# Every float32r matmul reads the two halves of its moving operand in turn

## The chip, the cores and the metric

The kernel runs on one core of one Trainium2 chip. The metric is the device time of one execution in microseconds (us); shown is the median of three executions. A profile of one further execution gives the durations that are read below; times in its rows are us unless marked ns. PE is the matmul engine (TensorE), PEld its weight load, which runs beside the matmuls; ACT is ScalarE, DVE VectorE, POOL GpSimd, SP the engine that starts the DMA transfers.

## The reference

Attention with a sigmoid in place of the softmax, and behind it a two-layer network with a squared ReLU. All inputs and outputs are float32.

```python
scores = scale * np.matmul(q, k.transpose(0, 1, 3, 2)) - np.log(S)   # 8 x 12 heads, S = 448, head_dim 64
attn = 1.0 / (1.0 + np.exp(-scores))
x = np.matmul(attn, v)            # -> 3584 tokens x 768
h = x @ w_in                      # 768 x 2048
r = np.maximum(h, 0.0)
out = (r * r) @ w_out             # 2048 x 768
```

## The kernel before

Precision comes from splitting. A float32 operand is cast to float32r, the fast matmul type, as a "hi" part (on ACT in `split_to`, L373, or on DVE, L566), and DVE subtracts that from the raw words for the "lo" part (L375, L377, L570). A product is then three float32r matmuls: hi by hi, hi by lo, lo by hi.

**Attention** (the first 246 us) goes over 24 blocks, function `block`; one block does two head pairs of one batch. A pair's two heads lie on partitions 0 to 63 and 64 to 127, so that the matmuls of the two heads run side by side. On PE a block is, in order: `scores_rest` (L322, 8 plain float32 matmuls for the last 64 keys of each head), `scores` of both pairs (L305, 36 float32r matmuls of 448 columns, that is 18 side-by-side pairs), then `attn_v` (L337) and `attn_v_rest` (L349) in plain float32. On ACT each of the score tiles passes through a sigmoid (L290): first the tile "rest", then six tiles "at". The sums of `attn_v` take the PSUM buffers that the sigmoids set free, in rotation over four. Beside that, ACT, DVE and POOL convert weights from 64-bit words and DVE adds up blocks for the matrix products.

**The two matrix products** use a seven-product (Strassen-like) scheme over halves of rows and columns, `gemm1` and `gemm2`, for four groups of tokens: three of 2 x 512 and a last one of 2 x 256 (`GROUPS`, T is 512 or 256). In the groups with T = 512 each matmul moves 512 columns: in `gemm1` the attention result (tiles xh, xl, xht, xlt, y, yt) against weights w1A to w1D, in `gemm2` the squared activations (tiles o_0h to o_3l). In the last group `gemm1` moves 256 columns (`product`), or, for products 2, 7 and 4, hi and lo side by side as 512 columns (L626) and then hi alone as 256 (L628, both in `joined_product`); `gemm2` is turned there: the activations are the stationary operand and the weights move, 384 columns at a time.

A moving operand of exactly 512 columns outside `joined_product` is read "woven" before the change: column 0 of the first half, column 0 of the second half, column 1 of the first, and so on. So that the result comes out in the plain order, `weave_to` and `split` write these operands with the raw words read at a step of two (even ones into the first half, odd ones into the second). All other matmuls read their moving operand from front to end, and their operands are split in plain order.

The order of the work is written out by hand for attention and for parts of the matrix products (`tc.manual_schedule`), and follows the program's order; PE results in `gemm1` are copied out of PSUM by ACT ("s", L688) before the next product adds onto the same bank.

Of the kernel before, what the change touches and what calls it, by code (L numbers as in the profile page):

```python
# [18 lines left out]
B, H, S, D = 8, 12, 448, 64  # L19
DM, DFF = H * D, 2048  # L20
P = 128
NP = H // 2

NT, KR = S // P, S % P
NF = DFF // P
NI = NF // 2
HALF = DM // 2
NE = HALF // P
GROUPS = ((0, 512), (1024, 512), (2048, 512), (3072, 256))
NG = len(GROUPS)  # L30
NS = 512
# [49 lines left out]
def sigmoid_attention_relu2_mlp(  # L81
# [47 lines left out]
    nc = tc.nc  # L129
# [3 lines left out]
    def op2(name, dtype=F32, n=S):  # L133
        return sb.tile([P, 2, n], dtype, tag="op2", bufs=N2, name=name)

    def op1(name, dtype=F32, n=S):
        return sb.tile([P, n], dtype, tag="op1", bufs=N1, name=name)
# [2 lines left out]
        return sb.tile([P, PH, HALF], dtype, tag="w", bufs=NW, name=name)  # L140

    def load_unit(src, u, name):
        t = wide(name).rearrange("p a n -> p (a n)")
        nc.sync.dma_start(out=t.bitcast(I32), in_=src[u].bitcast(I32))
        return t.rearrange("p (n w) -> p n w", w=2)
# [122 lines left out]
    def raw_of(half, k):  # L270
        if (half, k) not in raw_first:
            raw_first[half, k] = op2(f"x0_{half}{k}", n=NS), op1(f"y0_{half}{k}", n=NS)
        return raw_first[half, k]
# [14 lines left out]
    def sigmoid(name, sc):  # L288
        at = op2(name)
        nc.scalar.activation(at, sc, AF.Sigmoid, bias=NEG_LOG_S, scale=SCALE)  # L290
        return at

    def scores(b, p, x, passes=SPLIT, apart=0):

        sc, out = {}, []
        order = [range(apart), range(apart, len(passes))]
        for t, ns in [(t, order[0]) for t in range(NT) if apart] + [(t, order[1]) for t in range(NT)]:
            if t not in sc:
                sc[t] = two(f"sc_{b}_{p}_{t}")
            ks = slice(t * P, (t + 1) * P)  # L300
            for n in ns:
                kp, qp = passes[n]
                for j in range(2):
                    rows = slice(j * D, (j + 1) * D)
                    nc.tensor.matmul(  # L305
                        sc[t][:, j],
                        x[kp][rows, 1, ks],
                        x[qp][rows, 0],
                        start=(n == 0),
                        stop=(n == len(passes) - 1),  # L310
                    )
            if ns[-1] == len(passes) - 1:
                out.append(sigmoid(f"at_{b}_{p}_{t}", sc[t]))
        return out

    def scores_rest(d, xs):

        sc = two(f"sr_{d}")
        for r, x in enumerate(xs):
            for j in range(2):  # L320
                rows = slice(j * D, (j + 1) * D)
                nc.tensor.matmul(  # L322
                    sc[r * KR : (r + 1) * KR, j], x[rows, 1, NT * P :], x[rows, 0], start=True, stop=True
                )
        return sigmoid(f"rest_{d}", sc)

# [45 lines left out]
    def split_to(hi, lo, raw, later=None):  # L372
        nc.scalar.copy(out=hi, in_=raw)  # L373
        if later is None:
            nc.vector.tensor_sub(out=lo, in0=raw, in1=hi.bitcast(F32))  # L375
        else:
            later.append(lambda: nc.vector.tensor_sub(out=lo, in0=raw, in1=hi.bitcast(F32)))  # L377

    def unwoven(t, order):
        a = "a " if len(t.shape) > 2 else ""  # L380
        return t.rearrange(f"p {a}({order}) -> p {a}n s", n=2)

    def weave_to(hi, lo, raw, later=None):
        split_to(unwoven(hi, "n s"), unwoven(lo, "n s"), unwoven(raw, "s n"), later)

    def woven(t):
        return t.rearrange("p (n s) -> p s n", n=2)

    def split(raw, name, new):
        hi, lo = new(name + "h", F32R), new(name + "l", F32R)  # L390
        weave_to(hi, lo, raw)
        return hi, lo

    def x_operands(g):

        raw = {}
        t0, T = GROUPS[g]

        def load(n, b, k):
            if g == 0:
                raw[n] = raw_of(b, k)
                return
            r2, r1 = op2(f"x{n}_{g}", n=T), op1(f"y{n}_{g}", n=T)
            src = xd[3 * k : 3 * k + 3, :, t0 + b * T : t0 + (b + 1) * T].rearrange("c p s -> p c s")
            nc.sync.dma_start(out=r2, in_=src[:, 0:2])
            nc.sync.dma_start(out=r1, in_=src[:, 2])
            raw[n] = [r2, r1]

        def sub(n, a, b):
            for o, x, y in zip(raw[n], raw[a], raw[b]):
                nc.vector.tensor_sub(out=o, in0=x, in1=y)

        ops, ys = {}, {}

        def make(product, n, later=None, whole=False):
            if 2 * T > NS:
                y = op2(f"y{n}_{g}", F32R, T)
                h1, l1 = y[:, 0], y[:, 1]  # L420
                h2, l2 = (op2(f"{c}{n}_{g}", F32R, T) for c in ("xh", "xl"))
                ops[product] = [(h2[:, c], l2[:, c], None) for c in range(2)] + [(h1, l1, None)]
            else:
                x = op2(f"xj{n}_{g}", F32R, 2 * T)
                kind, at = SPOT[product]
                if kind not in ys:
                    ys[kind] = op2(f"yj{kind}_{g}", F32R, 2 * T)
                y = ys[kind][:, at]
                (h2, l2), (h1, l1) = ((t[..., :T], t[..., T:]) for t in (x, y))
                ops[product] = [(h2[:, c], l2[:, c], x[:, c]) for c in range(2)] + [(h1, l1, y)]  # L430
            (x2, x1) = raw[n]
            to = weave_to if 2 * T > NS else split_to
            to(h2, l2, x2, later)
            if whole:
                later.append(lambda: to(h1, l1, x1))
            else:
                to(h1, l1, x1, later)

        load("11", 0, 0)
        load("12", 1, 0)  # L440
        load("22", 1, 1)
        load("21", 0, 1)
        raw["t2"] = raw["22"] if g == 0 else [op2(f"xt_{g}", n=T), op1(f"yt_{g}", n=T)]
        raw["t1"], raw["t3"], raw["t4"] = raw["12"], raw["11"], raw["21"]
        return ops, {
            1: lambda *later: make(1, "11", *later),
            2: lambda *later: make(2, "21", *later),
            "t1": lambda: sub("t1", "12", "11"),
            "t2": lambda: sub("t2", "22", "t1"),
            6: lambda *later: make(6, "t2", *later),  # L450
            "t3": lambda: sub("t3", "t2", "11"),
            7: lambda: make(7, "t3"),
            5: lambda: make(5, "t1"),
            3: lambda *later: make(3, "22", *later),
            "t4": lambda: sub("t4", "21", "t2"),
            4: lambda: make(4, "t4"),
        }
# [5 lines left out]
    last = len(pairs) - 1  # L463
    todo = [(m, i) for m in range(2) for i in range(NI) if m == 0 or i not in DEFERRED]
    x, vt, xs, at, pav, xo, f64, w = {}, {}, {}, {}, {}, {}, {}, {}
    ready, stores, later, words = [], [], [], []
# [105 lines left out]
    def score(n, *args):  # L572
        at[n] = scores(*pairs[n], *args)
# [12 lines left out]
    first = {}  # L586
# [22 lines left out]
    def two(name):  # L609
        return duo(name, pools[next(turn) % 4])  # L610
# [4 lines left out]
    def product(out, w, c, x, first, last):  # L615
        (wh, wl), (xh, xl) = w, x
        for n, (a, b) in enumerate(((wh, xh), (wh, xl), (wl, xh))):
            moving = woven(b) if b.shape[-1] == NS else b
            nc.tensor.matmul(  # L619
                out, a[:, c], moving, start=first and n == 0, stop=last and n == 2, skip_group_check=True  # L620
            )

    def joined_product(out, w, xs, first):
        wh, wl = w
        for c, (*_, both) in enumerate(xs):
            nc.tensor.matmul(out, wh[:, c], both, start=first and c == 0, stop=c == NE - 1, skip_group_check=True)  # L626
        for c, (xh, *_) in enumerate(xs):
            nc.tensor.matmul(  # L628
                out[:, : xh.shape[-1]], wl[:, c], xh, start=False, stop=c == NE - 1, skip_group_check=True
            )  # L630

    def operand_of(g, raw, name, later=None):
        T = GROUPS[g][1]
        if 2 * T > NS:
            return (*split(raw, name, lambda *names: op2(*names, T)), None)
        both = op2(name, F32R, 2 * T)
        hi, lo = both[:, :, :T], both[:, :, T:]
        split_to(hi, lo, raw, later)
        return hi, lo, both
# [374 lines left out]
```

## Time and profile before

| | us |
|---|---|
| median of 3 executions | 1026.84 (1026.49 to 1028.62) |
| the profiled execution | 1027.23 |
| its span, first to last instruction | 1025.5 |
| PE busy in the span | 1018.4 (99%) |
| PEld, DVE, ACT, POOL busy | 821.8, 834.4, 711.3, 72.3 |
| granted clock of PE | 1.00 throughout |

A matmul's duration is longer than its share of PE's time, since consecutive matmuls overlap in the array. What a matmul costs is the step from its start to the next one's start: the chain of waits gives it for runs of equal matmuls (length of the run by their count), the timeline by the starts.

### The profile page before, as it was taken

To read this page: it belongs to the slowest core of one execution; us is meant where nothing else is said; L and a number is where in the kernel's file an instruction comes from. 1 tells how busy PE (TensorE), PEld (TensorE's weight loads), DVE (VectorE), ACT (ScalarE), POOL (GpSimd) and SP (SyncE) were. 2 spreads that over 40 slices of the span, in tenths; PEclk is the share of its full clock that TensorE was granted. 3 is DMA by queue.
4 is the path that set the end of the run, shared out by engine and by line. 5 is a ranking of instruction groups with operands and counts; after the bars stand their busy time and mean duration, and the time that the engine had idled before them with its cause. 6 is when DMAs were issued, how large, how long until landed. Compare 5 with 4: busy or idle time off the path is not lost.

```text
span 1025.5 us, 16201 instructions
## 1 busy us (share of the span) xinstructions
PE 1018.4 (99%) x6194; PEld 821.8 (80%) x6194; DVE 834.4 (81%) x1024; ACT 711.3 (69%) x917; POOL 72.3 (7%) x42
## 2 busy tenths in 40 slices
PE   9999999999999999999999999999999999999998
PEld 4555555556888888888888888888888888899998
DVE  5999999996788599977554899966555999759994
ACT  7889999987686686936443868555434869358763
POOL 1232231310121000000000000000000000000000
PEclk9999999999999999999999999999999999999999
DMA  9988999983566535544333436362333344566374
GB/s 362 397 309 301 377 381 356 352 280 110 195 216 197 156 95 164 191 143 136 96 104 104 121 117 208 95 222 82 108 106 110 106 155 148 182 203 229 112 201 124
DMA packets 90366, 196.11 MB, mean 191 GB/s; under 512 B 8240, under 2 KB 51504, under 8 KB 90288
## 3 DMA queue, kind: packets, MB, share of 16 engines
q1 hardware_dynamic: 90288, 195.07, 57.1%
q8 instruction: 49, 0.80, 0.3%
q14 instruction: 29, 0.24, 0.1%
HBM read 154.14 MB, written 40.89 MB: 190 GB/s over the span
## 4 chain that ended last, share of the span: by engine, by line
PE 95%; ACT 2%; DMA 1%; issue 0%; DVE 0%; SPq 0%; ACTq 0%
PE oa L619 21%; PE ha L619 20%; PE pav L337 11%; PE ob L619 11%; PE sc L305 9%; PE hb L619 8%; PE oc L619 5%; PE hc L619 4%; PE sr L322 2%; PE pav L349 2%; PE hb L626 1%; DMA w1A<-w 1%; DMA w1D<-w 1%; PE hb L628 1%; PE hc L626 1%
## 5 line engine op out<-in xcount | busy, mean ns | idle before, releaser
L290 ACT ACTIVATE at<-sc 128x896 f32<-128x896 f32 x144 | 119.3, 942 | 4.2 <-PE sc L305 4.2
L375 DVE TENSOR_TENSOR w<-w 128x768 fp32r<-128x768 f32 x108 | 103.5, 963 | 20.2 <-ACT w L373 20.2
L373 ACT CAST w<-w 128x768 fp32r<-128x768 f32 x108 | 90.4, 848 | 41.6 <-DMA w<-w 41.6
L337 PE MATMUL pav<-at,v 64*64 64x448 f32 x1152 | 118.1, 540 | 0.0
L688 ACT COPY s<-ha 128x512 f32<-128x512 f32 (+1 forms) x96 | 51.3, 534 | 93.9 <-PE ha L619 91.8
L337 PEld LDWEIGHTS pav<-at,v 64*64 64x64 f32 x1152 | 41.6, 133 | 60.8 <-issue 54.2
L570 DVE TENSOR_TENSOR ql<-x,qh 128x896 fp32r<-128x896 f32 x47 | 72.4, 1580 | 0.0
L172 POOL TENSOR_TENSOR a<-a,f 128x768 int32<-128x768 int32 x26 | 58.1, 2236 | 160.2 <-DVE a L169 86.5
L691 DVE TENSOR_TENSOR g<-hb,s 128x512 f32<-128x512 f32 (+1 forms) x64 | 39.6, 619 | 26.7 <-ACT s L688 22.8
L375 DVE TENSOR_TENSOR w1A<-w1A 128x768 fp32r<-128x768 f32 x24 | 22.9, 955 | 39.8 <-ACT w1A L373 39.6
L305 PE MATMUL sc<-qh 64*128 64x448 f32 x282 | 53.8, 380 | 0.0
L305 PE MATMUL sc<-ql,qh 64*128 64x448 f32 x282 | 51.4, 361 | 0.0
L305 PE MATMUL sc<-qh,ql 64*128 64x448 f32 x282 | 51.4, 361 | 0.0
L373 ACT CAST w1A<-w1A 128x768 fp32r<-128x768 f32 x32 | 26.7, 835 | 29.4 <-DMA w1A<-w 27.9
L619 PE MATMUL oa<-o_1h,w 128*128 128x512 f32 x144 | 44.9, 380 | 0.0
L619 PE MATMUL oa<-o_0h,w 128*128 128x512 f32 x144 | 44.8, 379 | 0.0
L619 PE MATMUL oa<-o_2h,w 128*128 128x512 f32 x144 | 44.8, 379 | 0.0
L619 PE MATMUL oa<-o_3h,w 128*128 128x512 f32 x144 | 44.8, 379 | 0.0
L305 PEld LDWEIGHTS sc<-qh 64*128 64x128 f32 x282 | 26.3, 184 | 19.1 <-PE pav L337 16.2
L671 DVE SCALAR_TENSOR_TENSOR g<-g 128x1024 f32<-128x1024 f32 (+1 forms) x34 | 38.4, 1130 | 1.1
L355 ACT COPY xo<-pav 128x448 f32<-128x448 f32 x48 | 25.6, 533 | 19.6 <-PE pav L349 10.9
L566 DVE CAST qh<-x 128x896 fp32r<-128x896 f32 x47 | 32.5, 729 | 6.8 <-DMA x<-qk 6.8
(315 smaller groups left out, 2837.9 us busy)
## 6 DMA issues: line engine op xcount, KB each, us to landing
w<-w SPq DMA_DIRECT2D x108, 384.0 KB, 3.3
x<-qk SPq DMA_DIRECT2D x47, 448.0 KB, 6.9
f<-w_in SPq DMA_DIRECT2D x16, 768.0 KB, 8.9
w1A<-w SPq DMA_DIRECT2D x32, 384.0 KB, 3.5
w1B<-w SPq DMA_DIRECT2D x31, 384.0 KB, 3.4
w1C<-w SPq DMA_DIRECT2D x31, 384.0 KB, 3.4
v<-v SPq DMA_DIRECT2D x24, 448.0 KB, 7.7
w<-s SPq DMA_DIRECT2D x26, 384.0 KB, 8.4
```

Of the source, the lines that this page charges most:

```text
L172: nc.gpsimd.tensor_tensor(out=wb, in0=wb, in1=t.bitcast(I32)[:, :, 0], op=ALU.add)
L290: nc.scalar.activation(at, sc, AF.Sigmoid, bias=NEG_LOG_S, scale=SCALE)
L305: nc.tensor.matmul(sc[t][:, j], x[kp][rows, 1, ks], x[qp][rows, 0], start=(n == 0), stop=(n == len(passes) - 1),)
L337: nc.tensor.matmul(sums[columns, h], vt[rows, n % 2 * NT + t, columns], at[t][rows, j], start=(t == 0 and (n % 2, h) != (1, 1)), stop=(t = ...
L373: nc.scalar.copy(out=hi, in_=raw)
L375: nc.vector.tensor_sub(out=lo, in0=raw, in1=hi.bitcast(F32))
L566: nc.vector.tensor_copy(out=xs[n][0], in_=x[n])
L570: nc.vector.tensor_sub(out=xs[n][1], in0=x[n], in1=xs[n][0].bitcast(F32))
L619: nc.tensor.matmul(out, a[:, c], moving, start=first and n == 0, stop=last and n == 2, skip_group_check=True)
L671: nc.vector.scalar_tensor_tensor(out=t, in0=t, scalar=0.0, in1=t, op0=ALU.max, op1=ALU.mult)
L688: nc.scalar.copy(out=s, in_=banks["a", i])
L691: nc.vector.tensor_add(out=to, in0=from_[:, :T], in1=s)
```

## The change

`woven` now serves every float32r matmul: scores of all kinds (L305, L322, which takes in the plain float32 ones there too), `product` at any width, and `joined_product`, where hi and lo are two runs with two halves each. The halves lie half the operand's columns apart: 256 columns (1024 bytes) at 512, 224 (896 bytes) at 448, 192 (768 bytes) at 384, 128 (512 bytes) at 256 and within each run of the joined operand. The splits (`split`, `make`) now go in plain order everywhere, and `unwoven` and `weave_to` are gone. Output columns are thus shuffled, once or twice, and the host puts them in order. No instruction is added, removed or put in another place on any engine.

```diff
+    def woven(t, runs=1):
+        if runs == 1:
+            return t.rearrange("p (n s) -> p s n", n=2)
+        return t.rearrange("p (h n s) -> p h s n", h=runs, n=2)
...
                         sc[t][:, j],
                         x[kp][rows, 1, ks],
-                        x[qp][rows, 0],
+                        woven(x[qp][rows, 0]),
...
-                    sc[r * KR : (r + 1) * KR, j], x[rows, 1, NT * P :], x[rows, 0], start=True, stop=True
+                    sc[r * KR : (r + 1) * KR, j], x[rows, 1, NT * P :], woven(x[rows, 0]), start=True, stop=True
...
-    def unwoven(t, order):
-        a = "a " if len(t.shape) > 2 else ""
-        return t.rearrange(f"p {a}({order}) -> p {a}n s", n=2)
-
-    def weave_to(hi, lo, raw, later=None):
-        split_to(unwoven(hi, "n s"), unwoven(lo, "n s"), unwoven(raw, "s n"), later)
-
-    def woven(t):
-        return t.rearrange("p (n s) -> p s n", n=2)
-
     def split(raw, name, new):
         hi, lo = new(name + "h", F32R), new(name + "l", F32R)
-        weave_to(hi, lo, raw)
+        split_to(hi, lo, raw)
...
-            to = weave_to if 2 * T > NS else split_to
-            to(h2, l2, x2, later)
+            split_to(h2, l2, x2, later)
...
-            moving = woven(b) if b.shape[-1] == NS else b
             nc.tensor.matmul(
-                out, a[:, c], moving, start=first and n == 0, stop=last and n == 2, skip_group_check=True
+                out, a[:, c], woven(b), start=first and n == 0, stop=last and n == 2, skip_group_check=True
             )
...
-            nc.tensor.matmul(out, wh[:, c], both, start=first and c == 0, stop=c == NE - 1, skip_group_check=True)
+            nc.tensor.matmul(
+                out, wh[:, c], woven(both, 2), start=first and c == 0, stop=c == NE - 1, skip_group_check=True
+            )
...
-                out[:, : xh.shape[-1]], wl[:, c], xh, start=False, stop=c == NE - 1, skip_group_check=True
+                out[:, : xh.shape[-1]], wl[:, c], woven(xh), start=False, stop=c == NE - 1, skip_group_check=True
```

## Rows read from the trace of the kernel before

**Rows 1.** The page: busy time, share of the span and instructions of each engine.

```profile
PE 1018.4 (99%) x6194; PEld 821.8 (80%) x6194; DVE 834.4 (81%) x1024; ACT 711.3 (69%) x917; POOL 72.3 (7%) x42
```

**Rows 2.** Windows (stretch, its length, then busy time of each engine): attention, gemm1, last gemm2.

```profile
15.80:246.15 230.35, 230.35 (x2304) 129.43 (x2296) 215.77 (x293) 206.50 (x268) 58.15 (x26) 1.00 0.90 333
246.15:356.40 110.25, 109.56 (x509) 95.34 (x506) 81.38 (x120) 78.70 (x112) 13.96 (x12) 1.00 0.57 178
465.00:575.00 110.00, 108.96 (x503) 94.60 (x503) 64.30 (x75) 51.30 (x76) 0.00 (x0) 1.00 0.37 107
...
962.50:1022.00 59.50, 59.48 (x344) 59.03 (x342) 47.58 (x72) 32.98 (x53) 0.00 (x0) 1.00 0.49 140
```

**Rows 3.** Chain of waits: start, length, engine, tile, line and count of a piece.

```profile
575.87 15.54 PE oa L619 x72
...
910.40 0.69 PE hc L626 x3
911.09 0.36 PE hc L628 x3
911.45 2.16 PE ha L619 x18
...
980.38 8.32 PE oa L619 x48
```

**Rows 4.** Timeline of PE, one attention block: start, length, operation, out<-in, shapes, count.

```profile
105.85 0.93 PE L322 MATMUL sr<-x 64*64 64x448 f32 x8
...
107.01 0.36 PE L305 MATMUL sc<-qh,ql 64*128 64x448 f32 x2
...
110.25 0.36 PE L305 MATMUL sc<-ql,qh 64*128 64x448 f32 x2
110.54 2.49 PE L337 MATMUL pav<-at,v 64*64 64x448 f32 x24
```

**Rows 5.** Timeline of ACT, the same block: the six sigmoids.

```profile
107.69 4.96 ACT L290 ACTIVATE at<-sc 128x896 f32<-128x896 f32 x6
```

**Rows 6.** Timelines of ACT and PE, the next block: sigmoids, first attn_v matmuls.

```profile
117.90 3.34 ACT L290 ACTIVATE at<-sc 128x896 f32<-128x896 f32 x4
120.55 0.98 PE L337 MATMUL pav<-at,v 64*64 64x448 f32 x8
```

**Rows 7.** Groups of weight loads (busy, mean ns): last group's gemm1, an earlier one's.

```profile
L619 PEld LDWEIGHTS ha<-xj,w1A 128*128 128x128 f32 x42 | 5.5, 192 | 0.0
...
L619 PEld LDWEIGHTS ha<-xh,w1A 128*128 128x128 f32 x20 | 3.8, 189 | 0.5
```

**Rows 8.** Groups on ACT: a split at step two, then passes in plain order.

```profile
L373 ACT CAST o_1h<-g 128x1024 fp32r<-128x1024 f32 x18 | 29.3, 1625 | 0.6 <-DVE g L843 0.5
...
L669 ACT ACTIVATE g<-g 128x1024 f32<-128x1024 f32 x20 | 21.2, 1058 | 0.5
L373 ACT CAST o<-g 128x512 fp32r<-128x512 f32 x24 | 14.3, 620 | 2.7 <-DVE g L671 2.2 <-DVE g L840 0.4
```

**Rows 9.** Waits of PE: who waited for whom, us in total, times, longest.

```profile
PE ha L619 <- ACT s L688: 2.2, 3, 0.8
...
PE hb L619 <- DVE w1D L375: 0.6, 2, 0.3
```

**Rows 10.** Timeline of ACT, start of the second group's gemm1, and before the other stall.

```profile
473.20 1.56 ACT L373 CAST xh<-x 128x1024 fp32r<-128x1024 f32 x1
474.65 0.81 ACT L373 CAST y<-y 128x512 fp32r<-128x512 f32 x1
475.34 0.60 ACT L688 COPY s<-ha 128x512 f32<-128x512 f32 x1
...
570.02 1.58 ACT L373 CAST o_0h<-g 128x1024 fp32r<-128x1024 f32 x1
```

**Rows 11.** Timeline of PE at the first of these two places.

```profile
474.42 0.81 PE L619 MATMUL ha<-y,w1A 128*128 128x512 f32 x3
476.00 0.48 PE L619 MATMUL ha<-xht,w1C 128*128 128x512 f32 x1 [0.77 <-ACT s L688]
```

More of the change, by code (lines that the diff above doesn't have):

```diff
@@ L431, in make @@
             (x2, x1) = raw[n]
-            to = weave_to if 2 * T > NS else split_to
-            to(h2, l2, x2, later)
+            split_to(h2, l2, x2, later)
             if whole:
-                later.append(lambda: to(h1, l1, x1))
+                later.append(lambda: split_to(h1, l1, x1))
             else:
-                to(h1, l1, x1, later)
+                split_to(h1, l1, x1, later)
         load("11", 0, 0)
@@ L1012, with places @@
     r = run_bass_kernel_spmd(nc, [arrays], core_ids=[0])
-    return np.concatenate([r.results[0]["outT"].T, r.results[0]["out_last"]])
+    def places(n):
+        return np.arange(n).reshape(2, n // 2).T.reshape(n)
+    tokens = (np.arange(B)[:, None] * S + places(S)).reshape(B * S)
+    tiles = tokens[:t0].reshape(-1, NS)[:, places(NS)[places(NS)]].reshape(t0)
+    rows = tokens[t0:].reshape(2, T)[:, places(T)].reshape(2 * T)
+    columns = (np.arange(2)[:, None] * HALF + places(HALF)).reshape(DM)
+    out = np.empty((B * S, DM), np.float32)
+    out[tiles] = r.results[0]["outT"].T
+    out[np.ix_(rows, columns)] = r.results[0]["out_last"]
+    return out
```

## The prediction

> **What bounds the kernel now.** I read the page's busy line first: PE is busy 1018.4 of 1025.5 us, the next engine 81% [rows 1]. The windows by stage then say whether that holds everywhere. It does: in attention PE is busy for all of 230.35 us, in the last group's gemm2 for 59.48 of 59.50, and only the gemm1 stages leave PE idle, 0.69 and 1.04 us [rows 2]. So time is gained by making PE's steps shorter or by taking away the few stalls of gemm1, and any engine that then gets close to its own limit decides how much is kept; DVE at 215.77 of 230.35 in attention is the nearest.
>
> Next, what a step costs. In an earlier group 72 woven matmuls of 512 columns take 15.54 us, 215.8 ns each; that is 0.4215 ns a column, and it is already woven. In the last group three joined matmuls of 512 columns, read from front to end, take 0.69, or 230 ns each; 18 of 256 columns take 2.16, or 120; three of L628 take 0.36, or 120; 48 of 384 take 8.32, or 173.3 [rows 3]. In attention a side-by-side pair of score matmuls takes (110.25 - 107.01) / 16 = 202.5 ns for 448 columns [rows 4]. At the woven rate these sizes would take 215.8, 107.9, 107.9, 161.9 and 188.8. Every plainly read float32r matmul thus costs 11 to 14 ns more than the woven rate, and the woven 512 shows none of that. Same shape, same kind of weight load, 230 against 215.8: the order of reading is the difference that I can see.
>
> **The change part by part.** No instruction is added, removed or moved, so that only durations change.
>
> *Scores.* 23 blocks have 18 pairs, the first has 9: 423 pairs. I take 190 ns a pair, 1 ns over the rate for the second matmul of a pair; that saves 12.5 ns, 0.225 us a block. What lies beside it: the attn_v matmuls behind the scores need the PSUM buffer of the third sigmoid. The six sigmoids start at 107.69 and take 4.96, in the next block four take 3.34, so 0.81 each, and the third of the block ends at 107.69 + 4.96 - 3 x 0.81 = 110.22 [rows 5, 6]. PE starts there at 110.54 [rows 4], 0.32 later. The closest that PE comes to it is in the next block, where a cast delays the chain: 117.90 + 3.34 - 0.81 = 120.43 against 120.55, 0.12 later [rows 6]. The sigmoid chain hangs on the float32 `scores_rest` ahead of it, which gets no faster. So the new start is bounded by 110.22 + 0.12 = 110.34, and of 0.225 us about 0.20 stay; in blocks with a cast ahead (I count two) nothing. 21 x 0.20 and 0.1 in the first block are 4.3; DVE, which would be busy 215.8 of some 226 us, I charge 0.2. Term: 4.1 us. Bounds: 5.3 (423 x 12.5) and 0.
>
> *The last group's gemm2.* 7 products x 48 matmuls = 336, from 173.3 to 161.9: 3.8 us. DVE is busy 47.58 of 59.5 there [rows 2], so PE at 55.7 still finds it under its limit.
>
> *Joined 512.* 3 products x 8 x 3 = 72, from 230 to 215.8: 1.0 us.
>
> *256 columns.* 4 x 8 x 9 = 288 in `product` and 72 in L628. At the woven rate each saves 12 ns, 4.3 us in all. But a weight load of 128 columns stands behind each matmul, and at this width nothing else of that matmul hides it. The load shows 192 ns here and 189 beside woven matmuls [rows 7]: if the load sets the step, only these 3 ns go, 1.1 us. I take 5 ns, 1.8 us, near the load's end because its row is the nearer one, and keep 1.1 and 4.3.
>
> The Trainium skill's "TensorE: Matmul & The Clock Gate", section "LDWEIGHTS (loading the stationary operand)", gives a weight load as its columns over 1.2 GHz; for 128 columns that makes an estimate of 107 ns. By that rule the load would not hold a step of 108 ns, and the sum would be 2.5 us lower than mine. The trace only has the loads' 192 and 189 ns with their latency, so it neither confirms nor refutes it.
>
> *Splits of the three big groups.* ACT's cast of 1024 elements at a step of two takes 1625 ns; a pass of the same shape in plain order takes 1058, and a plain cast of 512 takes 620 [rows 8]. PE hides nearly all of these casts, so that their 0.5 us each are worth nothing except where PE waits behind them. It does so five times, 2.2 us for copies "s" and 0.6 for w1D [rows 9]. The idle time understates them: at 474.42 three matmuls of 0.2158 start, the next is due at 475.07 and starts at 476.00, 0.93 late where the row says 0.77, and its first matmul lasts 0.48 instead of 0.38 [rows 11]. So each of the five costs 0.26 more than its idle time: 2.8 + 1.3 = 4.1 us. In front of that copy ACT runs a cast of xh, 1.56, and of y, 0.81 [rows 10]; in plain order 1.06 and 0.62, so the copy is ready 0.69 earlier and 0.24 of 0.93 remain. The stalls on w1D have one cast of 1.58 ahead on ACT [rows 10], 0.52 too long, which is more than what they wait. Over all five I keep 0.9 us of stall. Term: 3.2 us, bounds 4.1 and 1.5 (if the time won on ACT goes to the next wait on a weight transfer).
>
> *Plain float32 matmuls that are now woven too* (192 of `scores_rest`, 12 in the first block). Eight of them, four side by side at a time, hold PE for some 0.86 us before the first scores [rows 4], 0.43 for the same 448 columns, so they read at less than half the scores' rate and I take zero. No row shows them woven; bounded by the 7% that separates 202.5 from 188.8, 24 x 0.86 x 0.07 = 1.4 us either way.
>
> **Sum.** 4.1 + 3.8 + 1.0 + 1.8 + 3.2 = 13.9 us. The profiled execution took 1027.23, so 1013.3; against the median of 1026.84, 0.4 lower, 1012.9. I forecast 1013.0.
>
> **Rivals.**
>
> *The scores keep their price or attention hands it back* (1017.1). Pairs of 64-row matmuls are never woven in this trace, their halves lie 896 bytes apart and not 1024, and two weight loads run beside them. Or ACT, busy 206.5 us of 230, holds the block through the sigmoid chain, which has 0.32 us to give. For it: 0.12 us is all that is left in some blocks. Against it: 0.32 exceeds 0.225. It gives 1013.0 + 4.1.
>
> *The reading order is not the cause* (1023.8). The 11 to 14 ns would belong to what the last group and the scores have in common otherwise, more weight loads per column. For it: the excess at 256 and 384 columns is nearly the same 11 to 12 ns, as if it went with the load and not with the columns. Against it: 230 against 215.8 at equal width. Only the splits' 3.2 us would be left: 1027.0 - 3.2.
>
> *In-turn reading costs more at distances other than 1024 bytes* (1036). What shows woven reads as free has 1024 bytes between its halves; 896, 768 and 512 are not in the trace. If two halves at such distances hinder each other, each of these matmuls could pay its present excess twice: 5.3 + 3.8 + 1.0 + 2 to 4.3 are about 12.5 us more, less 3.2 for the splits, 1036. It decides from an excess that grows by a quarter, since that eats the 3.2 us. Against it: the 72 of the chain come from many buffers and run at 215.8 [rows 3] without a trace of hindrance.
>
> A rule that speaks for this last case stands in the Trainium skill, "SBUF — State Buffer", section "Specifications (TRN2)": lines of 16 bytes want at least two hits each for full bandwidth, and each move to a new line costs. Reading halves in turn goes to a new line with every column, and by the rule the woven matmuls should be the slow ones, at any distance. The trace disagrees, with 215.8 ns woven and 230 plain at 512 columns [rows 3], and the measurement decides; I give the case a chance only for the distances not shown.
>
> *More than I take* (1009.3): the 256-column matmuls go to the full rate and attention keeps all, 2.5 + 1.2 us more.
>
> **How the numbers follow.** Forecast 0.58, scores without gain 0.17, splits alone 0.10, slower 0.08, more than forecast 0.07. The range of 1008 to 1021 holds the forecast with its bounds (5.3 + 3.8 + 1.0 + 4.3 + 4.1 = 18.5 at best, 1008.3), the first rival and the fifth; it leaves out the two in which the in-turn reading fails, 0.18. A measurement of this kernel can tell about 0.2%, 2 us, from no change. Faster by that: 0.58 + 0.17 + 0.07 and about half of the splits-alone case, 0.87; the other half, 0.05, within it; slower 0.08.
>
> **What would show it.** In the chain of waits 48 matmuls of the last gemm2 should take 7.8 us instead of 8.32, three joined 0.65 instead of 0.69, 18 of 256 columns between 1.95 and 2.1 instead of 2.16. In attention the starts of score pairs should be 190 ns apart and a block some 9.8 us long, with the first attn_v matmul about 0.1 us behind the third sigmoid's end. ACT's casts of 1024 elements should take about 1.06 us, and the waits on copies "s" shrink to a third. Wrong would be: pairs at 200 ns or more, steps of 384 columns above 170, or a row of waits on ACT or DVE in every attention block.

## The result and the profile after

The changed kernel takes 1015.68 us (median of 4, 1015.51 to 1015.84) against 1026.78 before, with a fourth execution counted: a ratio of 0.9888, 95% interval 0.9871 to 0.9905. That lies in the forecast range; of the 13.9 us forecast, 11.1 came. The sum hides that attention gave far less than its term and the big groups more, which the stages show. Stage bounds are starts of the same matmuls in both profiles.

| stage | before | after | difference | forecast |
|---|---|---|---|---|
| start to the first gemm1 matmul (attention) | 246.27 | 244.70 | -1.57 | -4.1 |
| three big groups | 657.56 | 653.62 | -3.94 | -3.2 |
| last group, gemm1 to the first gemm2 matmul | 58.66 | 56.40 | -2.26 | -2.8 |
| last group, gemm2 to the end of the span | 62.96 | 59.20 | -3.76 | -3.8 |

The page of the changed kernel, answering to [rows 1]:

```profile
PE 1008.6 (99%) x6194; PEld 816.4 (81%) x6194; DVE 802.4 (79%) x1024; ACT 657.9 (65%) x917; POOL 72.1 (7%) x42
```

PE still bounds the kernel; ACT and DVE have 53 and 32 us less to do. The chain of waits after, answering to [rows 3] (start, length, engine, tile, line, count):

```profile
904.46 0.65 PE hc L619 x3
905.11 0.33 PE hc L623 x3
905.45 2.01 PE ha L612 x18
...
979.27 7.80 PE ob L612 x48
```

Steps of 384 columns went from 173.3 to 162.5 ns, joined 512 from 230 to 217, 256 columns from 120 to 112 (L612) and 110 (L623). In attention, the block of [rows 4]: its first score in the kernel before, then the timelines of PE and of ACT in the changed kernel:

```profile
106.71 0.47 PE L305 MATMUL sc<-qh 64*128 64x448 f32 x2
```

```profile
105.04 1.12 PE L327 MATMUL sr<-x 64*64 64x448 f32 x8
106.10 0.46 PE L310 MATMUL sc<-qh 64*128 64x448 f32 x2
106.39 0.35 PE L310 MATMUL sc<-qh,ql 64*128 64x448 f32 x2
...
109.42 0.35 PE L310 MATMUL sc<-ql,qh 64*128 64x448 f32 x2
109.70 2.49 PE L342 MATMUL pav<-at,v 64*64 64x448 f32 x24
```

```profile
107.08 4.96 ACT L295 ACTIVATE at<-sc 128x896 f32<-128x896 f32 x6
```

The float32r pairs now start (109.42 - 106.39) / 16 = 189 ns apart instead of 202.5. But the eight plain float32 matmuls ahead of them take 1.06 us from their first start to the first score instead of 106.71 - 105.85 = 0.86. So 18 pairs win 0.24 us a block, `scores_rest` takes back 0.19, and a block shrinks from 10.01 to 9.97. Where PE waits, and the DVE timeline at the first of those places:

```profile
PE ha L612 <- DVE w1A L382: 0.7, 1, 0.7
PE ha L612 <- ACT s L683: 0.4, 1, 0.4
```

```profile
936.59 0.69 DVE L666 SCALAR_TENSOR_TENSOR g<-g 128x512 f32<-128x512 f32 x1
937.20 0.95 DVE L382 TENSOR_TENSOR w1A<-w1A 128x768 fp32r<-128x768 f32 x1
```

The five waits of [rows 9] are gone (three of their places, and one more, keep about 0.1 us and a restart). Two new ones stand in the last group's gemm1. PE needs w1A at 937.35, and DVE, working without a gap, splits it from 937.20 on. PE goes on 0.86 us late:

```profile
938.21 0.71 PE L612 MATMUL ha<-xj,w1A 128*128 128x256 f32 x4 [0.69 <-DVE w1A L382]
```

The second wait is put down to ACT's copy "s". Timelines of PE there and of ACT, which ahead of that copy waited for DVE itself:

```profile
953.61 0.94 PE L612 MATMUL ha<-xj,w1C 128*128 128x256 f32 x6 [0.42 <-ACT s L683]
```

```profile
951.41 1.14 ACT L378 CAST o<-g 128x512 fp32r<-128x512 f32 x2 [0.77 <-DVE g L666]
```

The first group of [rows 8], now split in plain order:

```profile
L378 ACT CAST o_1h<-g 128x1024 fp32r<-128x1024 f32 x18 | 18.7, 1041 | 1.1 <-DVE g L838 1.1
```

### The profile page after: what moved, and what is told of

It reads as the page before. It is cut to its first block, busy times and chain, and to the rows that moved or that the text cites. A ratio compares the mean times of both kernels' runs of the same rounds, so it can differ in the third digit from the quotient of the medians.

```text
span 1013.9 us, 16201 instructions
## 1 busy us (share of the span) xinstructions
PE 1008.6 (99%) x6194; PEld 816.4 (81%) x6194; DVE 802.4 (79%) x1024; ACT 657.9 (65%) x917; POOL 72.1 (7%) x42
## 4 chain that ended last, share of the span: by engine, by line
PE 96%; DVE 3%; issue 1%; ACT 1%; DVEq 0%
PE oa L612 21%; PE ha L612 19%; PE pav L342 11%; PE ob L612 11%; PE hb L612 9%; PE sc L310 9%; PE oc L612 5%; PE hc L612 5%; PE sr L327 2%; PE pav L354 2%; DVE g L688 1%; DVE g L686 1%; DVE w1B L382 0%; DVE w1C L382 0%; PE warm_ps L914 0%
## 5 line engine op out<-in xcount | busy, mean ns | idle before, releaser
L612 PE MATMUL oa<-o_0h,w 128*128 128x512 f32 x144 | 44.8, 379 | 0.0
L612 PE MATMUL oa<-o_1h,w 128*128 128x512 f32 x144 | 44.8, 379 | 0.0
L612 PE MATMUL oa<-o_2h,w 128*128 128x512 f32 x144 | 44.8, 379 | 0.0
L612 PE MATMUL oa<-o_3h,w 128*128 128x512 f32 x144 | 44.8, 379 | 0.0
L378 ACT CAST w1B<-w1B 128x768 fp32r<-128x768 f32 x31 | 25.9, 836 | 20.5 <-DMA w1B<-w 19.5
```

The source lines that it names most:

```text
L612: nc.tensor.matmul(out, a[:, c], woven(b), start=first and n == 0, stop=last and n == 2, skip_group_check=True)
```

## The experiments

**Only the splits in plain order.** Scores and the last group read as before, and the host's order is fitted to that; the 512-column matmuls keep reading in turn.

```diff
-                        woven(x[qp][rows, 0]),
+                        x[qp][rows, 0],
...
-                out, a[:, c], woven(b), start=first and n == 0, stop=last and n == 2, skip_group_check=True
+                out, a[:, c], woven(b) if b.shape[-1] == NS else b, start=first and n == 0, stop=last and n == 2, skip_group_check=True
```

> Scores, the 256- and 384-column matmuls and the joined ones read from front to end as before; only the operands of the three big groups are split in plain order. Theory A (the time comes from the reading order of the float32r matmuls, and beside it from the shorter casts): the stalls of gemm1 in the big groups go, 3.9 us, so about 1022.9 us; pairs of scores at 202.5 ns, 384 columns at 173.3. Rival C (the reading order is not the cause, the casts alone are): 1015.7, as with the whole change.

Measured: 1022.36 us, ratio 0.9954 (0.9939 to 0.9969). PE's waits in gemm1 are gone; the last gemm2 keeps its old step. Chain of waits of this run:

```profile
975.42 8.32 PE oa L612 x48
983.74 8.32 PE ob L612 x48
```

The big groups take 653.62 us, to the last digit as in the changed kernel, and the last group's two stages 58.66 and 62.96 as before. So 3.9 us of the gain come from the splits in plain order, and the rest hangs on the reading order. The medians lie 4.9 us apart; in the profiles the further 1.0 us lies in the first attention block, whose length the next experiment shows to vary by chance. Theory A stands, and "the reading order is not the cause" is refuted.

**All scores from front to end again.** The same edit in `scores` and `scores_rest`, the last group as changed.

> The changed kernel, but all scores, scores_rest too, read from front to end as before. Theory A (in attention 5.7 us are won by the float32r pairs and 0.8 by the first block's plain float32 ones, and 4.6 us lost by scores_rest): attention ends at 246.3 us instead of 244.7, the time is 1017.3. Rival D (attention as a whole wins or loses nothing, all of the gain is behind it): 1015.7.

Measured: 1017.04 us, ratio 0.9899 (0.9882 to 0.9915), 1.4 us over the changed kernel. The blocks say more than that time does: the profiled execution, the longest of the four, also spent 4.90 us behind its last matmul against 3.45 in the changed kernel, which the edit does not touch. Blocks are back at 10.01 us, and the 23 of them (from 15.32 to 245.73) take 230.4 us as before, against 229.4 (15.34 to 244.70) in the changed kernel: 1.0 us, about what 18 x 13.5 ns less 0.19 us make over 23 blocks (1.2). The part on the first block was wrong. Timeline of PE, its 12 plain float32 matmuls, in the kernel before, the changed kernel, this run and `splits_only`:

```profile
3.69 3.92 PE L305 MATMUL sc<-x 64*128 64x448 f32 x12
```

```profile
3.69 3.41 PE L310 MATMUL sc<-x 64*128 64x448 f32 x12
```

```profile
3.69 3.45 PE L310 MATMUL sc<-x 64*128 64x448 f32 x12
```

```profile
3.69 2.92 PE L310 MATMUL sc<-x 64*128 64x448 f32 x12
```

Three of the four read from front to end and differ by a microsecond. Their pairs step by some 740 ns at first and by 374 later, and the moment of the change differs from profile to profile (granted clock 1.00 in each window there); no row says why. Once past it, a pair read in turn steps by 473. The half microsecond by which the first block was shorter after the change is thus chance, and attention's part of the gain is 1.0 us, not 1.57. D is refuted, narrowly, by the blocks.

**scores_rest from front to end, the rest as changed.**

```diff
-                    sc[r * KR : (r + 1) * KR, j], x[rows, 1, NT * P :], woven(x[rows, 0]), start=True, stop=True
+                    sc[r * KR : (r + 1) * KR, j], x[rows, 1, NT * P :], x[rows, 0], start=True, stop=True
```

> The changed kernel, but the plain float32 matmuls of scores_rest read from front to end again; the last 64 keys are thereby added to other columns than the first 384. Theory A (these matmuls pay for the in-turn reading, 0.19 us a block): scores_rest back from 1.05 to 0.86 us, a block at 9.78 instead of 9.97, 24 x 0.19 = 4.5 us less at most, about 1011.3 us. Rival B (attention is held by the chain of sigmoids, and the longer scores_rest only fills a wait that would be there anyway): a block stays at 9.97 and the time at 1015.7, with PE waiting for ACT ahead of attn_v in every block.

Measured: 1014.27 us, ratio 0.9875 (0.9860 to 0.9890). Neither theory's number. `scores_rest` is back at its old length, and nine blocks take exactly the 9.78 us of theory A, so B falls. But the others take 9.79 to 10.6, and 1.6 of 4.5 us are kept. The waits of PE and the timeline of a stretched block (PE, then DVE):

```profile
PE sc L310 <- DVE xo L374: 0.7, 2, 0.6
```

```profile
125.91 0.46 PE L310 MATMUL sc<-qh 64*128 64x448 f32 x2 [0.55 <-DVE xo L374]
```

```profile
124.77 0.55 DVE L189 TENSOR_TENSOR s<-a,s 128x384 f32<-128x384 f32 x1
125.24 1.15 DVE L374 TENSOR_TENSOR xo<-pav,xo 128x448 f32<-128x448 f32 x2
126.30 1.15 DVE L560 CAST qh<-x 128x896 fp32r<-128x896 f32 x2
```

PE waits for a PSUM buffer that the DVE adds of L374 set free, and these stand behind the sums of weights on a DVE without gaps. That says DVE, but it is one place; the next run tests it.

**The same, with less for DVE.** The clamp of the weight words is left out.

```diff
-        nc.vector.tensor_scalar(out=w, in0=w, scalar1=WORD_MIN, scalar2=WORD_MAX, op0=ALU.max, op1=ALU.min)
```

> The kernel in which scores_rest reads from front to end again (1014.27 us), with one DVE pass of 0.55 us left out of each weight conversion, the clamp of the words, 26 passes in attention and 12 shorter ones behind it. Theory G (with PE at 9.78 us a block, DVE is what stretches blocks to 9.9 to 10.6): the stretched blocks shrink towards 9.78, attention ends 2 us or more earlier, 1011.5 to 1012.3. Rival H (the stretched blocks wait for ACT's chain or for loads): no more than 0.3 us less, 1014.

Measured: 1011.91 us, ratio 0.9845 (0.9828 to 0.9861). Windows over the 23 blocks, `rest_plain` first, then this run:

```profile
15.06:243.07 228.01, 227.24 (x2304) 128.85 (x2296) 217.81 (x293) 206.10 (x268) 57.98 (x26) 1.00 0.92 339
```

```profile
15.06:240.74 225.68, 225.68 (x2309) 130.15 (x2301) 196.39 (x267) 206.20 (x268) 57.98 (x26) 1.00 0.91 341
```

With 21.4 us less on DVE and ACT as busy as before, the stretch is 2.33 us shorter and PE has no idle time: 9.81 us a block. G holds: at a PE block of 9.78, DVE is the limit at 217.8 of 228 us, though it is "only" 95.5% busy. In the changed kernel DVE is 94% busy over the same stretch and its blocks of 9.97 are not stretched:

```profile
15.34:244.70 229.36, 229.36 (x2304) 130.11 (x2297) 216.03 (x293) 205.80 (x268) 57.92 (x26) 1.00 0.90 336
```

**Six reading orders.** The operand's columns are rearranged by place:

```diff
+    def order(t, how):
+        if how == "plain":
+            return t
+        if how == "step two":
+            return t.rearrange("p (s n) -> p n s", n=2)
+        if how == "quarters":
+            return t.rearrange("p (n s) -> p s n", n=4)
+        runs = {"halves": 1, "runs of 2": 2, "runs of 4": 4}[how]
+        return t.rearrange("p (n s r) -> p s n r", n=2, r=runs)
```

> One look at six reading orders, told apart by place: scores_rest by block (block d takes order d mod 6), the float32r scores by block too (blocks 0-3, 4-7 and so on), the last gemm2 by product; orders: front to end, halves in turn, halves in turn by runs of 2 columns, by runs of 4, step two (even columns, then odd), quarters in turn. The last gemm2's product 4 reads from front to end with weights of 64 columns instead of 128, and product 5 of the third group's gemm2 reads its 512 columns from front to end. The order of tokens and features is mixed by that, and half of product 4 is left out. Theory A1 (the excess of float32r comes from reading one line of neighbouring columns after the other; reading two places in turn takes it away): front to end 173 and 202, 16.6 us for 72 matmuls of 512 columns instead of 15.5; halves and quarters 162 and 189; runs of 4 fall back to 173 and 202; 64-column weights still 173. Theory A2 (the excess is a clash with the weight load that runs beside the matmul): 64-column weights at 168 or less, and runs of 2 and 4 still at 162, since two places are read. For the plain float32 of scores_rest, theory A: every order but front to end takes about 0.47 us for four matmuls, front to end 0.38; rival E (only two far-apart places cost): step two at 0.38 as well.

Measured once: 1062.38 us, which means nothing by itself. The chain of waits; the last gemm2's products from the second on read halves, runs of 2, runs of 4, step two, front to end with 64-column weights, quarters; the piece before them is the end of the first (front to end), the one at 880.06 the 512-column product from front to end:

```profile
880.06 16.35 PE oa L624 x72
...
986.08 7.13 PE oa L624 x41
993.21 7.80 PE oc L624 x48
1001.01 11.85 PE oa L624 x48
1012.87 9.18 PE ob L624 x48
1022.04 16.93 PE oa L624 x48
1038.97 8.32 PE ob L624 x48
1047.29 9.87 PE oa L624 x48
```

The timeline of PE, `scores_rest` by block: halves, runs of 2, runs of 4, step two, quarters:

```profile
15.50 1.12 PE L339 MATMUL sr<-x 64*64 64x448 f32 x8
25.71 0.97 PE L339 MATMUL sr<-x 64*64 64x448 f32 x8
35.76 0.93 PE L339 MATMUL sr<-x 64*64 64x448 f32 x8
45.77 0.97 PE L339 MATMUL sr<-x 64*64 64x448 f32 x8
55.58 1.71 PE L339 MATMUL sr<-x 64*64 64x448 f32 x8
```

| order | float32r, 384 columns, ns | float32r pair, 448, ns | four plain float32, 448, ns |
|---|---|---|---|
| front to end | 173 | 203 | 376 |
| halves in turn | 162.5 | 189 | 469 |
| runs of 2 in turn | 247 | 287 | 397 |
| runs of 4 in turn | 191 | 213 | 376 |
| step two | 353 | 395 | 396 |
| quarters in turn | 206 | 238 | about 750 |

(384: piece by count; the other two: median step between starts.) A2 falls: half the weight columns change nothing, 173.3. A1 falls too: quarters read from several places and cost 206, and runs of 4 do not fall back to 173 but go past it. What holds is narrower: of these six, reading two halves column by column is the one order that float32r takes at the full rate. For plain float32 the order of merit is another one: front to end and runs of 4 are best, halves cost a quarter more. Theory A's 0.47 for every other order fails as well, and rival E is refuted in its number (step two costs 5%, not nothing). Why the orders cost what they cost stays open. At 512 columns front to end takes 227 in a big group, against 215.8.

**Two splits of the last group later.**

```diff
-LAST_SECOND = (8, 24, 15), (15, 31, 22), (22, 45, 29), (29, 50, 36)
+LAST_SECOND = (8, 24, 15), (15, 31, 22), (22, 45, 53), (29, 50, 55)
```

> The changed kernel with two splits of weights for the last gemm2 (768 elements, 0.95 us of DVE each) moved from the middle of the last gemm1 to its end, where they are first needed some 4 and 6 us later. Theory A (the last group's gemm1, shortened by the in-turn reading, runs into DVE; two stalls of 0.86 and 0.59 us with their restarts cost 1.4 us): both stalls go or shrink, 1.0 to 1.4 us less, 1014.4. Rival F (the stalls come from weights that land late, not from DVE's queue): 1015.7.

Measured: 1014.30 us, ratio 0.9870 (0.9855 to 0.9885). The timeline of PE at the place of the first stall:

```profile
936.75 0.28 PE L623 MATMUL hb<-yjD,w1D 128*128 128x256 f32 x1
936.86 0.90 PE L612 MATMUL ha<-xj,w1A 128*128 128x256 f32 x6
```

The six matmuls run through, with 0.07 us lost; the second stall is gone as well. 1.4 us, as theory A said, with the loads left as they were: DVE's queue made both stalls, the second by way of ACT.

**scores_rest from front to end, put in order by its sigmoid.** On top of the late splits, a version that keeps all outputs in place:

```diff
+        nc.scalar.activation(
+            at.rearrange("p a (s n) -> p a n s", n=2),
+            sc.rearrange("p a (n s) -> p a n s", n=2),
+            AF.Sigmoid,
+            bias=NEG_LOG_S,
+            scale=SCALE,
+        )
```

> The kernel with the two late splits (1014.3 us), but scores_rest reads from front to end and the sigmoid on its result puts the columns in order, by writing its 2 x 448 columns at a step of two. If the step costs ACT nothing, scores_rest gives its 0.19 us a block back and DVE holds part of it, as with scores_rest read plainly: 1.4 us less, 1012.9. If it costs ACT as much as reading SBUF at a step of two did in the casts (1625 against 1058 ns), the sigmoid tile rest takes 1.4 us instead of 0.92, the chain of sigmoids ends 0.45 us later and attn_v waits for it in every block: a block at 10.2 us, 1020.

Measured: 1012.97 us, ratio 0.9860 (0.9844 to 0.9877): 2.7 us below the changed kernel's median, with no overlap of their runs, and the fastest version here that leaves nothing out. That is the first of the two cases. The group on ACT, in the changed kernel and in this one:

```profile
L295 ACT ACTIVATE rest<-sr 128x896 f32<-128x896 f32 x24 | 22.1, 919 | 9.3 <-PE sr L327 9.3
```

```profile
L331 ACT ACTIVATE rest<-sr 128x896 f32<-128x896 f32 x24 | 24.6, 1023 | 5.1 <-PE sr L327 5.1
```

Writing at a step of two costs this sigmoid 0.10 us, not the half more that reading at a step of two cost the casts. The chain of sigmoids has most of that to spare: in the block that starts at 104.19 us, attn_v starts 4.50 us after the block's first matmul, against 4.47 in the same block of `rest_plain`; over the blocks that DVE does not stretch there, it starts 0.01 to 0.08 us later.

## Why the prediction was right, and where it was not

That the time fell into the range is partly luck and the range's width, which allowed the scores' term to be nothing: attention came 2.5 us short of its 4.1, or 3.1 without the first block's chance, and the splits' 0.7 above their term hid part of that.

**Scores: the step that failed.** "Pairs at 190 ns" was right (189). The prediction then took the plain float32 matmuls that are woven too as zero, bounded by 1.4 us either way; `scores_rest` cost 24 x 0.19 = 4.6 us, three times the bound. The reason given was that they read at less than half the scores' rate, and the bound of 7% was taken from float32r rows. The six orders show that the two types do not share a price list: halves cost float32 469 instead of 376 ns for four (the prediction's 0.43 us included the change to the next kind of matmul). The first block's plain scores pay by the same measure, 473 instead of 374 ns a pair, though the profiles' chance hides it.

**Attention's limit.** "0.20 of 0.225 stay" rested on the chain of sigmoids, with attn_v about 0.1 us behind the third one. That is what the profile shows: 107.08 + 4.96 - 3 x 0.81 = 109.61, and attn_v at 109.70. But DVE was charged 0.2 us in all. At the block length forecast it costs some 3 us: `rest_plain` needs 228.0 us where 23 x 9.78 are 224.9, and giving DVE less work took 2.3 of these away. So even without the cost of `scores_rest` the term would have come out near 2.5, not 4.1. The forecast saw DVE at 215.8 of 226 us and took the rest for slack; the run shows that at 217.8 of 228 there is none.

**Last gemm2**: 3.8 forecast, 3.76 measured; DVE stayed under its limit there as said. **Joined 512**: 217 where 215.8 was taken.

**256 columns**: 1.8 was taken, on the idea that the weight load might set the step. It does not hold it at the 115 taken: steps of 112 and 110 are worth about 2.9 us, between the 1.8 and the 4.3 of the full rate. The Trainium skill's "TensorE: Matmul & The Clock Gate", section "LDWEIGHTS (loading the stationary operand)", gives a load as its columns over 1.2 GHz, by estimate 107 ns for 128 columns; the trace agrees in so far as steps of 110 and 112 are reached. The loads' own durations did not move (192 and 189 ns in the changed kernel, too), so these rows never said what the load costs in a stream. 1.4 us of the 2.9 went into the two new stalls that DVE causes, which the prediction did not have: it looked at DVE in gemm2 and not in gemm1.

**Splits**: 3.2 forecast, 3.9 measured; casts at 1.05 us as read from a plain pass. Of the five stalls 0.7 us is left where 0.9 was kept; the other half microsecond comes from stops of 0.1 to 0.2 us between matmuls of the big groups, which the list of waits does not show.

**The rivals.** The first rival's sum (1017.1) lies nearer to the measured time than the forecast, yet not for its reasons: the pairs do win at 896 bytes, and what attention hands back goes to plain float32 and not to ACT's chain. The case that in-turn reading costs more at other distances is refuted for float32r at 896, 768 and 512 bytes; plain float32 pays at the same 896 at which float32r gains, so there the type decides. The Trainium skill's "SBUF — State Buffer", section "Specifications (TRN2)", wants two hits or more for each line of 16 bytes. Read as in the prediction, it is contradicted further: runs of 4 columns, by that rule a whole line at a time, are slower (191) than halves with one hit per visit (162.5), and step two, two hits per line, is slowest (353).

## What to carry to other kernels

A change of access pattern has a price per data type and form, not per engine: list every instruction whose operand changes, and for each form that the trace does not show, keep the bound wide or measure it by itself before summing. When the bounding engine is to get 2% faster, compare the new length with every other engine's busy time stage by stage, and do not take the last few per cent for slack: here DVE cost nothing at 94% and 3 us of 228 at 95.5%. An operand's order can be mended where an engine has slack, as the sigmoid's write shows.

## What the hardware showed beyond that

- Plain float32 pays about a quarter for halves in turn at both widths of weights: 376 to 469 ns for four matmuls of 64 by 64, 374 to 473 for a pair of 64 by 128. float32r gains 6 to 7% from the same order.
- float32r at a step of two takes 0.92 ns a column, 2.2 times the full rate; the order of reading alone moves a float32r matmul between 162 and 353 ns at 384 columns.
- ACT reads SBUF at a step of two at 1625 ns per 1024 elements against 1041 in order (the casts to o_1h), but writes at a step of two for 0.10 us more per 896.
